# First batch in passes of 128, 128 and 320 rows, channel mix opened by two chunks of 128 rows: top-k attention with a channel mix on one Trainium2 core

## The chip, the cores and the metric

The kernel runs on one core of one Trainium2 chip. Five engines of the core matter here, each with its own queue of instructions: PE (TensorE: matrix products and transposes), ACT (ScalarE), DVE (VectorE), POOL (GpSimd), and SP (SyncE), which issues nearly all transfers. They meet only through semaphores. The metric is the device time of one execution in microseconds (us), lower being better. The profile is of one execution; its span runs from the first to the last instruction of the core.

## The reference, cut to what matters

```python
def _attn_ref(q, k, v):                     # each 8 batches x 8 heads x 576 rows x 64
    scores = (1 / np.sqrt(64)) * np.matmul(q, k.transpose(0, 1, 3, 2))
    kth = np.partition(scores, -32, axis=-1)[..., -32:-31]
    scores = np.where(scores >= kth, scores, -1000000000.0)
    attn = np.exp(scores - np.max(scores, axis=-1, keepdims=True))
    attn = attn / (np.sum(attn, axis=-1, keepdims=True) + 1e-09)
    return np.matmul(attn, v)

def _moe_ref(x, mu_k, mu_r, w_k, w_v, w_r):  # x: 8 x 576 x 512; w_k 512x1024, w_v 1024x512, w_r 512x512
    x_prev = ...                             # x moved down by one row, zeros in the first
    xk = mu_k * x + (1.0 - mu_k) * x_prev
    xr = mu_r * x + (1.0 - mu_r) * x_prev
    k = np.maximum(xk @ w_k, 0.0)
    v = k * k @ w_v
    r = 1.0 / (1.0 + np.exp(-(xr @ w_r)))
    return r * v
```

The output of the attention, its heads side by side, is the x of the channel mix. A row of x is complete only when all eight heads of its batch have given that row.

## The kernel before, in words

**Attention.** A batch has 576 query rows and eight heads in four head pairs. The unit of work is a tile: 128 query rows of one head against all 576 keys. Tiles 0 to 7 of a head pair are four blocks of 128 rows, each for the two heads in turn; tile 8 holds the last 64 rows of both heads. Eight batches, four head pairs and nine tiles make 288 tiles. `visits` (line 56) lists in what order they are taken: a batch is cut into passes (`HALVES`, line 52: tiles 0 to 3, then 4 to 8, so 256 and 320 rows; `EDGE`, line 53, can give other cuts for single batches and is empty), and a pass runs over the four head pairs. One head pair within one pass is a visit; there are 64.

A visit brings in on the SP queue the rows beyond 512 of the keys (`tl`), its query rows (`qn`) and the values (`v`, `vr`); the first visit of a head pair also loads and transposes the keys (`kn`, `K`), which are then held for its later pass. Transposes are done on PE (lines 934 and 948) and copied out by ACT (939 and 950). For a tile, PE makes scores (`score`, line 990, and `sliver`, 986), ACT copies them to `sc` (995), DVE looks for the 32 largest (`cand`, 1000 to 1005), ACT and POOL count (1020, 1022), DVE finds the eighth candidate and the threshold (1023, 1025), ACT exponentiates (1028), DVE masks and sums (`mask`, 1031). PE then transposes the masked scores (1036), ACT copies them (1038), and PE multiplies by the values (`weigh`, 1066 and 1067). For up to four tiles of a visit together, DVE inverts the sums (`inv`, 1077 and `inv2`, 1078), POOL spreads them (1084), PE and ACT turn them (1088, 1093), and DVE writes the rows of x (`place`, 1101 and 1103).

**Weights.** The three weight matrices come in 20 blocks of 128 x 512, all near the start: each is split into two parts of reduced precision by ACT, four DVE operations (`wclamp`, `wshift`, `wsign`, `wexp`, lines 1280 to 1284) and POOL; twelve also use PE (1293). The last ones, for w_v, end on POOL (1298).

**Channel mix.** The 4608 output rows are cut into chunks (`SIZES`, line 70: 18 chunks of 256). POOL and ACT mix a chunk with its shifted rows and split it (lines 1173 to 1187); PE then does `hidden` (8 pieces of 12 products, moving operand as wide as the chunk), `gate` (2 pieces of 6 products, 512 wide, for each 128 rows) and `value` (4 such pieces for each 128 rows). Line 703 to 705 are the three products of the helper `three` that all pieces use. ACT and POOL bring `hidden` out (1202 to 1207), ACT and POOL work on the gate (1220 to 1224), DVE joins gate and value (1238, 1239), and SP stores. The buffers `hh` and `hl` for the hidden layer exist once, so a chunk's values must be done before the next chunk's hidden layer is written. The pieces of all chunks are chained one behind the other on PE (`piece`).

**Order.** All operations are put down as a graph with costs, and a planner (`Plan.run`, line 242) writes out one order for each engine before the kernel is built. It takes the operation that can start first, and among those that can start nearly as soon the one with the lowest key. A key is the number of the tile to which the work belongs plus a constant for the kind of operation (`OFF`, with `HEAD` added below key 48 and `TAIL` above 252). The key of a chunk follows from the number of the tile that completes its rows:

```python
at, size = at + STEP * size / CH, n
r = max(ready[b, u] for b, s, m in pieces for u in units_of(b, s, m)) + min(LAG, LAG0 + c * LAG1)
at = max(at, r)
```

A piece is also held back (`pace`, with PACE = -2) until the scores of the tile two before its key have been put in order. Readiness is 15 for the first 256 rows of the first batch and 35 for its other rows; STEP is 15.812 and LAG 10.811. So the first chunk has the key 15 + 8.92 = 23.9, the second 35 + 10.811 = 45.8, the third 51 + 10.811 = 61.8.

Of the kernel before, what the change touches and what calls it, by code (L numbers as in the profile page):

```python
# [37 lines left out]
OFF = dict(kt=-21.382, kq=-14.248, rest=-18.039, v=-7.011, v8=8.546, tk=-6.103, ck=5.233, tq=-5.229, cq=-6.609, tr=-1.299, cr=-10.196, zero=24.959,  # L38
           score=-0.141, score8=-16.328, keep=-1.042, cand=4.797, best=-8.27, drop=-27.489, under=-2.864, nb=-4.48, count=2.291, below=0.265,
           eighth=6.343, nine=7.479, exps=3.115, mask=-0.613, turn=3.366, et=4.204, turnl=3.568, el=4.37, weigh=1.271, inv=3.182, inv2=-5.081,  # L40
           turni=-0.009, ri=0.848, place=-1.878, lowest=20.12, ranks=16.635, mu=-6.363, nmu=11.593, changek=8.781, sharek=-2.615, addk=-15.155,
           xhk=-0.563, xlk=-31.338, changer=-9.67, sharer=8.479, addr=2.956, xhr=5.904, xlr=-8.649, hidden=2.062, relu=-10.213, sq=4.638, r2=6.141,
           hl=-4.223, gate=1.884, gexp=5.081, ga=14.727, ln=-4.806, inv1=3.806, newton=-5.08, value=-0.042, scaled=-17.152, gated=-15.006,
           store=7.854, w=19.648, wabs=-0.882, wclamp=0.952, wshift=-8.969, wsign=-1.393, wexp=-0.548, wfine=1.179, whi=3.694, wmul=8.819,
           wsub=-8.872, wlo=4.08, spread=1.597, sliver=-4.179, low=2.901, lowt=-13.42, lowr=-9.695, lowc=-4.212, wcp=0.231)
CANDS, BESTS = 0.045, -0.62
LAG, STEP, WAT, WSTEP, GATE, VALUE, PACE = 10.811, 15.812, 0.678, 0.755, 7.749, 14.045, -2.0
# [36 lines left out]
HEAD = dict(sharek=3.354, ck=-3.568, zero=6.524, lowt=3.202, score8=0.214, ga=4.843, store=3.315, el=0.191, gate=0.108, wlo=0.364, tr=-0.131,  # L84
            turni=-1.056, sq=3.388, ln=-4.07, hl=-5.431, changer=2.017, relu=-14.934, wmul=-1.439, low=4.872, xhk=0.716, inv=2.094, v=4.81,
            gated=-1.266, xlk=12.101, turn=0.113, r2=0.637, xlr=-10.187, inv1=4.923, addr=1.519, ri=-4.935, below=-1.831, scaled=-5.097, best=-1.072,
            wabs=-0.847, lowr=-0.696, sliver=-1.103, tk=-0.128, nmu=-3.551, kq=3.958, changek=2.107, count=-0.05, hidden=-1.273, addk=-5.101,
            xhr=2.146, lowc=-0.428, cq=0.701, eighth=-1.645, w=1.074, nb=-2.325, kt=-7.062, wshift=-2.765, wexp=0.003, ranks=8.978, rest=-10,
            spread=5.051, mask=-0.34, whi=0.196, newton=-10.373, drop=-2.508, gexp=-0.274, keep=-0.268, tq=-0.017, inv2=3.214, mu=-5.036, weigh=0.017,
            cr=-1.986, turnl=0.004, score=-0.211, under=-2.424, v8=2.951, nine=0.151, place=1.785, sharer=3.985, et=0.015, wfine=-0.129, wsign=1.009,  # L90
            exps=-0.306, wsub=-1.021, lowest=-1.465, value=0.017, wcp=-0.278)
TAIL = dict(addr=0.853, cr=4.328, wshift=-2.172, wexp=-2.611, scaled=0.049, sq=2.406, lowt=1.029, sliver=-0.332, nb=2.118, whi=1.277, xlk=6.06,
            xhk=3.07, store=0.534, nine=0.364, best=-3.303, wclamp=-3.212, ck=-0.471, rest=7.98, lowr=3.739, ln=-0.612, hl=2.336, turni=-5.416,
            xhr=-5.491, relu=-1.983, kt=0.597, v8=1.982, drop=-9.156, gate=-0.048, score8=3.803, eighth=1.269, under=5.06, inv2=2.762, v=0.064,
            w=-0.347, wmul=-2.191, wfine=2.635, cq=-0.832, lowest=-2.842, gexp=0.175, score=0.034, sharek=-1.259, wabs=-0.36, exps=0.582, nmu=-3.842,
            below=0.883, changek=2.733, tr=2.248, lowc=-0.397, tq=-0.647, wsub=1.611, inv=-0.862, low=2.896, gated=1.923, turnl=-0.233, place=1.226,
            ri=-4.487, r2=5.335, weigh=1.024, spread=-7.381, kq=3.792, cand=0.342, value=0.124, hidden=-0.65, newton=5.24, changer=2.918, zero=1.577,
            ranks=-4.862, mu=2.617, count=2.536, mask=4.85, tk=1.419, wsign=0.085, xlr=3.997, wlo=-3.068, inv1=-0.011, keep=-0.009, addk=4.321,
            ga=1.91, el=0.034, sharer=-1.07, wcp=0.415, turn=-0.048)
# [1349 lines left out]
```

## Time and profile before

| | |
|---|---|
| median of 3 runs | 1239.97 us (1239.73 to 1240.59) |
| the profiled execution's own time | 1239.58 us |
| its span | 1238.0 us |
| mean granted clock of TensorE | 0.981 |
| busy shares of the span | PE 96%, DVE 91%, ACT 89%, POOL 79% |

The span is 1.58 us shorter than the execution's own time, which includes what lies before its first and after its last instruction. A row of the windows view gives, for each stretch of the span, the busy time of every engine with the number of its instructions, the granted clock of TensorE, the mean share of the 16 transfer engines in use and the rate. A row of the grouped lines gives source line, engine, operation, output and input, shape, count, busy time and mean duration, then the idle time just before them. A mask of line 1031 leaves two records for each tile, the operation and the read of its sum, so records there are halved to count tiles. The chain of waits follows the work that ended last back in time.

### The profile page before, as it was taken

The page shows a single profiled execution, that of the slowest core. Times are in us where ns is not written, and L with a number is a line of the kernel's source. Part 1 is how long each engine was busy: PE and PEld are TensorE (multiplying, and loading weights), DVE is VectorE, ACT ScalarE, POOL GpSimd, SP SyncE. Part 2 cuts the span into 40 slices and gives each one's busy share as a digit, 9 for nine tenths or more (in the row PEclk, how much of TensorE's full clock was granted, in tenths as well). Part 3 has the DMA queues.
Part 4 walks back from the last instruction along what each step waited for, and adds up shares of the span by engine and source line. Part 5 has one row for each costly group of instructions (what it writes and reads, how often), then busy time and mean ns, then how long its engine had stood idle before and what let it go on. Part 6 is the DMA issues. An engine that isn't in the chain of part 4 may idle for free.

```text
span 1238.0 us, 29646 instructions
## 1 busy us (share of the span) xinstructions
PE 1185.3 (96%) x9069; PEld 913.8 (74%) x9069; DVE 1132.4 (91%) x6217; ACT 1107.8 (89%) x2428; POOL 980.6 (79%) x872
## 2 busy tenths in 40 slices
PE   5876999999999999999999999999999999999997
PEld 3434777878777776778787877787878787878786
DVE  5999999999999999999999999999989998999711
ACT  6897899999999999999999999999999999999752
POOL 2568995887778877888789787979697969788895
PEclk8997799999999999999999999999999999999999
DMA  7233112111221122111121112111211121101000
GB/s 189 93 95 97 35 35 66 41 36 42 57 54 31 45 50 57 36 39 45 50 56 38 35 49 58 42 43 34 59 47 45 27 59 40 50 26 32 20 27 20
DMA packets 125512, 61.80 MB, mean 50 GB/s; under 512 B 101792, under 2 KB 118176, under 8 KB 125344
## 3 DMA queue, kind: packets, MB, share of 16 engines
q1 hardware_dynamic: 124656, 59.42, 17.8%
q8 instruction: 74, 1.21, 0.4%
q14 instruction: 94, 0.77, 0.2%
q10 hardware_dynamic: 688, 0.39, 0.1%
HBM read 50.34 MB, written 9.44 MB: 48 GB/s over the span
## 4 chain that ended last, share of the span: by engine, by line
PE 79%; DVE 9%; ACT 6%; issue 1%; POOL 0%; DMA 0%; SPq 0%; DVEq 0%; ACTq 0%
PE rot L703 13%; PE rot L705 12%; PE rot L704 12%; PE ps L1066 10%; PE rot L1036 9%; PE ps L990 9%; PE ps L986 2%; PE ps L1067 2%; PE ps L977 2%; PE rot L934 2%; DVE cand L1000 2%; DVE E L1031 2%; PE rot L1088 1%; ACT sc L995 1%; PE ps L1045 1%; ACT se L1028 1%
## 5 line engine op out<-in xcount | busy, mean ns | idle before, releaser
L1022 POOL TENSOR_TENSOR sg<-sc,sg 128x576 f32<-128x576 f32 x288 | 409.2, 1423 | 165.6 <-ACT sg L1020 161.9
L1000 DVE MAX8 cand<-sc 128x8 f32<-128x82 f32 (+1 forms) x2016 | 390.5, 231 | 10.6 <-ACT sc L995 9.9
L1020 ACT ACTIVATE sg<-sc,seen 128x576 f32<-128x576 f32 x288 | 225.9, 784 | 8.6 <-DVE seen L1012 7.2
L1031 DVE SCALAR_TENSOR_TENSOR E<-sc,seen,se 128x576 f32<-128x576 f32 x288 | 231.0, 802 | 0.5 <-DVE nine L1025 0.2
L1028 ACT ACTIVATE se<-sc,seen 128x576 f32<-128x576 f32 x288 | 217.6, 756 | 8.4 <-DVE E L1031 5.8
L1023 DVE MAX8 top<-sg 128x8 f32<-128x576 f32 x288 | 215.7, 749 | 9.7 <-POOL sg L1022 9.2
L995 ACT ACTIVATE sc<-ps 128x576 f32<-128x576 f32 x288 | 185.4, 653 | 27.8 <-DVE E L1031 11.4
L1036 PE MATMUL rot<-ident,E 128*128 128x128 f32 x1152 | 180.7, 280 | 12.7 <-DVE E L1031 5.1
L1038 ACT ACTIVATE et<-rot 128x512 f32<-128x512 f32 x288 | 173.9, 604 | 9.7 <-PE rot L1036 8.6
L1002 DVE MAX8 top<-cand 128x8 f32<-128x56 f32 x864 | 179.7, 208 | 2.1
L1036 PEld LDWEIGHTS rot<-ident,E 128*128 128x128 f32 x1152 | 133.4, 143 | 62.6 <-DVE E L1031 7.1
L703 PE MATMUL rot<-xh,wk 128*128 128x256 f32 x576 | 172.5, 299 | 0.4 <-ACT kd L950 0.4
L1066 PEld LDWEIGHTS ps<-et,v 128*64 128x64 f32 x2560 | 128.7, 138 | 54.5 <-ACT el L1047 17.9
L1066 PE MATMUL ps<-et,v 128*64 128x128 f32 (+1 forms) x2560 | 164.4, 271 | 3.0 <-ACT el L1047 2.7
L705 PE MATMUL rot<-xh,wk 128*128 128x256 f32 x576 | 162.4, 282 | 0.0
L704 PE MATMUL rot<-xl,wk 128*128 128x256 f32 x576 | 162.1, 281 | 0.0
L990 PE MATMUL ps<-K,qs 64*128 64x512 f32 x512 | 149.7, 662 | 0.7 <-ACT sc L995 0.6
L703 PE MATMUL rot<-wv,hh 128*128 128x512 f32 x288 | 123.3, 428 | 0.0
L1005 DVE MATCH_REPLACE8 cand<-top,cand 128x56 f32<-128x56 f32 x576 | 115.9, 201 | 0.0
L705 PE MATMUL rot<-wv,hl 128*128 128x512 f32 x288 | 113.7, 395 | 0.0
L704 PE MATMUL rot<-wv,hh 128*128 128x512 f32 x288 | 113.6, 394 | 0.0
L703 PEld LDWEIGHTS rot<-xh,wk 128*128 128x128 f32 x576 | 109.7, 190 | 5.0 <-issue 2.4
(115 smaller groups left out, 2723.0 us busy)
## 6 DMA issues: line engine op xcount, KB each, us to landing
v<-in_v SPq DMA_DIRECT2D x64, 256.0 KB, 2.8
out<-eb SPq DMA_DIRECT2D x35, 256.0 KB, 2.0
kn<-in_k SPq DMA_DIRECT2D x64, 128.0 KB, 2.8
qn<-in_q SPq DMA_DIRECT2D x126, 64.0 KB, 2.1
stage<-in_moe_w_k SPq DMA_DIRECT2D x8, 512.0 KB, 6.2
xT<-in_moe_w_v SPq DMA_DIRECT2D x8, 512.0 KB, 3.6
tl<-in_k SPq DMA_DIRECT2D x128, 16.0 KB, 2.0
vr_in<-in_v SPq DMA_DIRECT2D x128, 16.0 KB, 2.5
```

Source lines behind the costliest of these rows:

```text
L703: return [nc.tensor.matmul(ps, lhsT=sh, rhs=mh, start=first, stop=False), nc.tensor.matmul(ps, lhsT=sh, rhs=ml, start=False, stop=False), ...
L704: nc.tensor.matmul(ps, lhsT=sh, rhs=ml, start=False, stop=False),
L705: nc.tensor.matmul(ps, lhsT=sl, rhs=mh, start=False, stop=last)]
L990: return [nc.tensor.matmul(ps[h].t, lhsT=qs.t[w, c * 128:(c + 1) * 128], rhs=P.K.t[w], start=True, stop=True) for h, w in enumerate(ws)]
L1000: lambda T=T, c=c: nc.vector.max(T.cand.t[:, 8 * c:8 * c + 8], T.sc.t[:, CUTS[c]:CUTS[c + 1]]), reads=[T.sc], writes=[(T.cand, c)])
L1020: lambda T=T, sn=sn: nc.scalar.activation(T.side.t, T.sc.t, AF.Sign, bias=sn(T, 1), scale=-BELOW, accum_out=T.top.t[:, TOPK:TOPK + 1]),
L1022: plan.op(POOL, "below", n, 1375, 1430, lambda T=T: nc.gpsimd.tensor_mul(T.side.t, T.sc.t, T.side.t), reads=[T.sc], writes=[T.side])
L1023: plan.op(DVE, "eighth", n, 660, 754, lambda T=T: nc.vector.max(T.top.t[:, 24:32], T.side.t), reads=[T.side], writes=[(T.top, 3)])
L1028: plan.op(ACT, "exps", n, 667, 754, lambda T=T, pe=pe, sn=sn: nc.scalar.activation(pe.t, T.sc.t, AF.Exp, bias=sn(T, 0), scale=SCALE), read ...
L1031: lambda T=T, U=U, pe=pe, sn=sn: nc.vector.scalar_tensor_tensor(T.e(), T.sc.t, sn(T, 2), pe.t, op0=OP.is_ge, op1=OP.mult, accum_out=U.rs.t ...
L1036: return [nc.tensor.transpose(pt.t[:, c * 128:(c + 1) * 128], E.t[:, o + c * 128:o + (c + 1) * 128], ident) for c in range(NKC)]
L1066: return [*[nc.tensor.matmul(pa[hs[j]], lhsT=vs[j][:, c, :], rhs=ms[c][j], start=(c == 0), stop=False) for c in range(NKC) for j in range(2)],
```

## The change

The first batch is cut into three passes instead of two: tiles 0 and 1 (rows 0 to 127), tiles 2 and 3 (rows 128 to 255) and tiles 4 to 8 (rows 256 to 575), each over all four head pairs. That makes 68 visits in place of 64. The first 256-row chunk of the channel mix becomes two of 128 rows; the other 17 chunks keep their rows. All constants of the planner's keys are given anew for this, so the order on every engine is another one over the whole kernel. No operation gets another form beyond the sizes that follow from the cuts.

```diff
-OFF = dict(kt=-21.382, kq=-14.248, rest=-18.039, v=-7.011, v8=8.546, tk=-6.103, ck=5.233, tq=-5.229, cq=-6.609, tr=-1.299, cr=-10.196, zero=24.959,
...
+OFF = dict(kt=-22.637, kq=-11.82, rest=-20.526, v=-9.532, v8=9.111, tk=-5.962, ck=8.211, tq=-5.193, cq=-8.242, tr=-1.288, cr=-9.428, zero=26.367,
...
-CANDS, BESTS = 0.045, -0.62
-LAG, STEP, WAT, WSTEP, GATE, VALUE, PACE = 10.811, 15.812, 0.678, 0.755, 7.749, 14.045, -2.0
+CANDS, BESTS = 0.044, -0.596
+LAG, STEP, WAT, WSTEP, GATE, VALUE, PACE = 10.811, 15.812, 0.129, 0.92, 7.756, 14.051, -2.0
...
-EDGE = {}
+EDGE = {0: (range(0, 2), range(2, 4), range(4, 9))}
...
-SIZES = [256, 256, 256, 256, 256, 256, 256, 256, 256, 256, 256, 256, 256, 256, 256, 256, 256, 256]
+SIZES = [128, 128, 256, 256, 256, 256, 256, 256, 256, 256, 256, 256, 256, 256, 256, 256, 256, 256, 256]
...
-BONUS = {("S", "W"): -1.086, ("T", "W"): 3.287, ("R", "W"): 3.489, ("T", "S"): -0.028, ("R", "S"): -0.426, ("W", "S"): -1.169, ("S", "R"): 1.769, ("T", "R"): -0.968, ("W", "R"): 4.451, ("R", "R"): -0.294}
+BONUS = {("S", "W"): -1.286, ("T", "W"): 3.343, ("R", "W"): 3.487, ("T", "S"): 0.148, ("R", "S"): -0.304, ("W", "S"): -1.2, ("S", "R"): 1.763, ("T", "R"): -0.968, ("W", "R"): 3.166, ("R", "R"): -0.386}
...
-NEAR = dict(PE=182, ACT=165, DVE=28, POOL=271, SP=294)
+NEAR = dict(PE=182, ACT=165, DVE=28, POOL=267, SP=505)
...
-LWAT, LWSTEP = -2.585, 1.51
-LAG0, LAG1 = 8.92, 24.398
+LWAT, LWSTEP = -2.439, 1.485
+LAG0, LAG1 = 9.28, 19.088
...
-HEAD = dict(sharek=3.354, ck=-3.568, zero=6.524, lowt=3.202, score8=0.214, ga=4.843, store=3.315, el=0.191, gate=0.108, wlo=0.364, tr=-0.131,
...
+HEAD = dict(sharek=-2.489, ck=-6.619, zero=11.997, lowt=6.27, score8=1.224, ga=1.872, store=16.832, el=0.208, gate=-0.08, wlo=-0.016, tr=0.09,
...
-TAIL = dict(addr=0.853, cr=4.328, wshift=-2.172, wexp=-2.611, scaled=0.049, sq=2.406, lowt=1.029, sliver=-0.332, nb=2.118, whi=1.277, xlk=6.06,
...
+TAIL = dict(addr=-4.273, cr=4.021, wshift=-3.452, wexp=-4.841, scaled=4.193, sq=1.982, lowt=0.079, sliver=-8.219, nb=-5.556, whi=-0.937, xlk=8.216,
...
```

More of the change, by code (lines that the diff above doesn't have):

```diff
@@ L37 @@
 BIG = 3.0e38
-OFF = dict(kt=-21.382, kq=-14.248, rest=-18.039, v=-7.011, v8=8.546, tk=-6.103, ck=5.233, tq=-5.229, cq=-6.609, tr=-1.299, cr=-10.196, zero=24.959,
[L39 to L45, printed above, removed]
@@ L78 @@
 WINDOW, PHASE, WARM, COLD = 3413.0, 2079.0, 0.87, 0.58
-NEAR = dict(PE=182, ACT=165, DVE=28, POOL=271, SP=294)
+NEAR = dict(PE=182, ACT=165, DVE=28, POOL=267, SP=505)
 LAST, JOINT, PEAT = "last", True, 112
-LWAT, LWSTEP = -2.585, 1.51
-LAG0, LAG1 = 8.92, 24.398
+LWAT, LWSTEP = -2.439, 1.485
+LAG0, LAG1 = 9.28, 19.088
 WPE = 12
-HEAD = dict(sharek=3.354, ck=-3.568, zero=6.524, lowt=3.202, score8=0.214, ga=4.843, store=3.315, el=0.191, gate=0.108, wlo=0.364, tr=-0.131,
[L85 to L91, printed above, removed]
@@ L92 @@
-TAIL = dict(addr=0.853, cr=4.328, wshift=-2.172, wexp=-2.611, scaled=0.049, sq=2.406, lowt=1.029, sliver=-0.332, nb=2.118, whi=1.277, xlk=6.06,
[L93 to L99, printed above, removed]
+HEAD = dict(sharek=-2.489, ck=-6.619, zero=11.997, lowt=6.27, score8=1.224, ga=1.872, store=16.832, el=0.208, gate=-0.08, wlo=-0.016, tr=0.09,
+            turni=-1.957, sq=-2.744, ln=4.584, hl=-11.257, changer=3.109, relu=-14.215, wmul=1.015, low=13.241, xhk=4.504, inv=0.63, v=2.378,
+            gated=-6.033, xlk=19.736, turn=0.098, r2=7.625, xlr=6.041, inv1=5.892, addr=3.26, ri=-4.602, below=1.293, scaled=-2.104, best=2.34,
+            wabs=-2.653, lowr=-15.341, sliver=-1.315, tk=-1.739, nmu=1.364, kq=-2.115, changek=1.165, count=0.39, hidden=-0.946, addk=-16.072,
+            xhr=5.643, lowc=0.912, cq=1.236, eighth=-1.334, w=2.16, nb=-19.454, kt=-8.364, wshift=-7.503, wexp=-0.768, ranks=-0.573, rest=-8.761,
+            spread=3.633, mask=-3.1, whi=0.215, newton=-13.635, drop=6.545, gexp=0.8, keep=0.344, tq=0.603, inv2=-0.157, mu=-5.336, weigh=0.135,
+            cr=4.349, turnl=0.369, score=-0.122, under=1.423, v8=2.742, nine=0.052, place=3.564, sharer=2.346, et=0.018, wfine=0.496, wsign=1.149,
+            exps=-0.453, wsub=-2.521, lowest=-13.921, value=1.331, wcp=-11.617, cand=-0.022)
@@ new lines @@
+TAIL = dict(addr=-4.273, cr=4.021, wshift=-3.452, wexp=-4.841, scaled=4.193, sq=1.982, lowt=0.079, sliver=-8.219, nb=-5.556, whi=-0.937, xlk=8.216,
+            xhk=1.771, store=6.443, nine=-0.18, best=-1.616, wclamp=0.814, ck=-0.469, rest=7.277, lowr=2.974, ln=-7.81, hl=2.432, turni=-8.13,
+            xhr=-2.471, relu=0.278, kt=-4.493, v8=3.31, drop=-14.733, gate=0.303, score8=2.521, eighth=1.07, under=1.611, inv2=7.305, v=4.437,
+            w=1.208, wmul=-1.261, wfine=5.003, cq=-1.045, lowest=-1.352, gexp=-0.071, score=-0.026, sharek=-0.433, wabs=-4.683, exps=2.021,
+            nmu=-4.225, below=2.677, changek=0.13, tr=1.919, lowc=-2.236, tq=-0.583, wsub=-3.633, inv=-8.16, low=-0.806, gated=13.198, turnl=-0.195,
+            place=-1.505, ri=1.021, r2=2.891, weigh=1.447, spread=-10.049, kq=2.911, cand=-0.026, value=0.71, hidden=-0.005, newton=7.797,
+            changer=2.951, zero=4.963, ranks=-8.616, mu=-7.588, count=-0.664, mask=-2.56, tk=5.532, wsign=-0.027, xlr=4.181, wlo=-5.593, inv1=0.946,
+            keep=-1.135, addk=1.419, ga=-3.618, el=0.17, sharer=7.791, wcp=1.202, turn=-1.67, et=-2.455)
```

7 lines of the change are left out of this document (added).

## The prediction

> **What bounds the kernel now.** I read the page's slices first, then the busy times by stage, then how many tiles each stage finishes.
>
> ```profile
> PE   5876999999999999999999999999999999999997
> ...
> DVE  5999999999999999999999999999989998999711
> ...
> PEclk8997799999999999999999999999999999999999
> ```
>
> Each digit covers 31 us. DVE is full from the second slice on, PE only from the fifth. The last three slices belong to PE alone. So I cut the span at 30, 100, 137, 222 and 1166 us and asked the windows view (columns: stretch, its length, busy time with count of PE, PEld, DVE, ACT, POOL, then granted clock, transfer share, GB/s).
>
> ```profile
> 0.00:30.00 30.00, 16.53 (x58) 9.38 (x58) 17.43 (x88) 17.68 (x35) 6.70 (x17) 0.84 0.70 185
> 30.00:100.00 70.00, 54.63 (x278) 28.52 (x276) 69.41 (x290) 61.19 (x128) 43.05 (x36) 0.94 0.35 103
> 100.00:137.00 37.00, 26.30 (x151) 17.11 (x152) 36.05 (x169) 30.57 (x64) 31.75 (x28) 0.68 0.25 73
> 137.00:222.00 85.00, 83.11 (x672) 65.26 (x671) 83.79 (x478) 79.56 (x180) 69.72 (x62) 0.98 0.18 44
> 222.00:1166.00 944.00, 939.08 (x7507) 736.80 (x7507) 914.17 (x5173) 889.84 (x1971) 776.45 (x691) 1.00 0.16 43
> 1166.00:1232.00 66.00, 65.61 (x411) 56.78 (x409) 11.24 (x25) 28.93 (x55) 52.90 (x43) 1.00 0.06 21
> ```
>
> The same view for the masks alone (line 1031, DVE, two records a tile):
>
> ```profile
> 30.00:100.00 70.00, 9.12 (x23) 0.94 0.35 103
> 100.00:137.00 37.00, 5.42 (x14) 0.68 0.25 73
> 137.00:222.00 85.00, 18.66 (x46) 0.98 0.18 44
> 222.00:1166.00 944.00, 197.69 (x488) 1.00 0.16 43
> ```
>
> Three regimes follow. From 30 to 222 us DVE bounds: it idles 0.59, 0.95 and 1.21 us in the three stretches, 2.75 us together. PE idles 37 - 26.30 = 10.7 us from 100 to 137, at a clock of 0.68. From 137 to 222, 23 tiles take 85 us, 3.70 us each. From 222 to 1166, 244 tiles take 944 us, 3.87 each, with PE idle for only 4.9 us and DVE for 29.8: there PE bounds. After 1166 the rest of the mix runs on a full PE.
>
> The mix begins here (source view: count, min/median/max duration, first and last start; then the first product of the second chunk in the timeline):
>
> ```profile
> L703 PE MATMUL rot<-xh,wk x576: 277/281/562, 136.7 to 1214.3; 128*128 128x256 f32 x192
> ```
>
> ```profile
> 209.92 0.38 PE L703 MATMUL rot<-xh,wk 128*128 128x256 f32 x1 [0.37 <-ACT kd L950]
> ```
>
> Chunk 0 thus fills PE from 137 us on, and chunk 1 starts at 210 us, about where its key 45.8 less the pace of 2 puts it.
>
> **The change part by part.** *Keys.* By the rule quoted above the prediction, the two small chunks get the keys 7 + 9.28 = 16.3 and 15 + 10.811 = 25.8 where the one had 23.9. The chunk with rows 256 to 511 keeps 45.8 (readiness 35), and so does every later one. So nothing of the mix after about 210 us moves against the tiles. The gain from starting early, if there is one, must come before that point, where DVE bounds.
>
> *PE.* I need the price of a product with 128 moving columns. The first two rows are neighbours of a hidden piece at full clock, the next two of a value piece (timeline, starts first), the last two the chain's time for four transposes and for one float32 product with 128 columns (both halves of it).
>
> ```profile
> 139.91 0.28 PE L703 MATMUL rot<-xh,wk 128*128 128x256 f32 x1
> 140.03 0.28 PE L704 MATMUL rot<-xl,wk 128*128 128x256 f32 x1
> ```
>
> ```profile
> 200.56 0.40 PE L703 MATMUL rot<-wv,hh 128*128 128x512 f32 x1
> 200.79 0.39 PE L704 MATMUL rot<-wv,hh 128*128 128x512 f32 x1
> ```
>
> ```profile
> 142.51 0.44 PE rot L1036 x4
> 144.92 0.22 PE ps L986 x2
> ```
>
> Start to start: 0.12 us for 256 columns, 0.23 for 512. For 128 columns the ends are half of the first, 0.06, and 0.22, the float32 product. I take 0.11, a transpose's 0.44 / 4, because it too loads 128 x 128 new weights for 128 columns. A 256-row chunk costs 96 x 0.12 + 24 x 0.23 + 48 x 0.23 = 28.1 us. A 128-row one costs 96 x 0.11 + 12 x 0.23 + 24 x 0.23 = 18.8 us. Two make 37.7, so PE gets 9.6 us more to do, and four more transposes of key rows, 0.44 us. Of chunk 0, hidden and gate (10.6 + 2.8 = 13.3 us) can run before 137 us; I leave its values after it, since they need w_v. Free there is 10.7 us at the clock of 0.68, so at least 7.3 us of full-speed work. At full clock today's 26.3 us would shrink to about 17.9 and leave 19.1. I take 13.3 as moved. What is left for 137 to 222 is 24.4 us against 28.1 now: PE is relieved there by 3.7 us, while DVE sets the pace.
>
> For the spacing of matrix products there is a page of the Trainium skill, "TensorE: Matmul & The Clock Gate", section "Back-to-back issue gap": a stream of weight loads with 128-column products is given about 81 ns a product. By it the two half chunks would cost 5.6 us less on PE; since DVE bounds that stage, the sum would stay as it is. No run here has shown such a product yet.
>
> *DVE.* Four more visits close four more groups.
>
> ```profile
> L1101 DVE TENSOR_TENSOR xT<-ps,ri 128x256 f32<-128x256 f32 x64 | 26.6, 416 | 3.2 <-PE ps L1067 0.9 <-POOL xm L1183 0.8 <-PE ps L1045 0.6
> L1078 DVE RECIPROCAL rs<-rot 128x4 f32<-128x4 f32 x64 | 10.6, 166 | 0.0
> L1077 DVE TENSOR_SCALAR rot<-rs 128x4 f32<-128x4 f32 x64 | 10.1, 158 | 0.6 <-ACT qs L939 0.4
> L1103 DVE TENSOR_TENSOR xT<-ps,ri 128x64 f32<-128x64 f32 x32 | 7.0, 218 | 2.2 <-ACT ri L1094 1.0 <-PE ps L1067 0.4 <-ACT sc L995 0.4
> ```
>
> Four times 0.158 + 0.166 is 1.3 us. A placement of 128 columns is, between 218 ns for 64 and 416 for 256, about 284 (an estimate); eight of them in place of four of 416 add 0.6. Together 1.9 us, all before 137 us, on the engine that bounds. Gate and value work on DVE stays at one pair for each 128 rows.
>
> In return PE is lighter from 137 on and earlier warm, so part of DVE's 2.75 us of waiting can go: at least nothing, at most all. I take two thirds, 1.8 us, because most of it lies after 100 us, where PE changes.
>
> *ACT, POOL, SP.* For each new visit ACT gets a copy of key rows at 0.279 us, and its copy of 256 query columns at 0.388 becomes two of 128, near 0.279 each.
>
> ```profile
> L939 ACT ACTIVATE qs<-rot 128x256 f32<-128x256 f32 x63 | 24.4, 388 | 2.0 <-PE rot L934 1.5
> L950 ACT ACTIVATE kd<-rot 128x128 f32<-128x128 f32 x32 | 8.9, 279 | 2.1 <-PE rot L948 1.9
> ```
>
> That is 4 x 0.45 = 1.8 us, and about as much again for the split mix, against 8.8 + 6.4 us of idle ACT from 30 to 137. Cost: nothing; without that cover, up to 4 us. SP issues four more sets of transfers:
>
> ```profile
> 9.54 0.47 SPq L920 DMA_DIRECT2D v<-in_v  x1
> 10.05 1.12 SPq L923 DMA_DIRECT2D vr_in<-in_v  x2
> 12.61 1.21 SPq L915 DMA_DIRECT2D tl<-in_k  x2
> ```
>
> At 2.8 us a visit this is 11 us of issue within the first 100, beside the weights' 20 blocks, which queue on SP too. Key loads of the four head pairs are wanted after two tiles each instead of four. I take nothing. The ends are -1 us (the first query load is half as large) and +3 us (a weight block or a key tile late while transfers are at 0.70 in the first 30 us). POOL is a rival below.
>
> *Sum.* Against the execution's own time: 1239.58 + 1.9 - 1.8 = 1239.7, and 0 for the stretches from 222 us on, whose keys and PE work are unchanged. The median lies 0.4 above that execution: **1240.0 us**, no change. For the new constants I take nothing either: no row prices another order. Their ends are bounded in the first rival.
>
> **The rivals.** *The new order carries the PE-bound stretch better (faster).* If its 244 tiles went at the 3.70 us of the stretch before, they would take 903 us, 41 less. So there is much to win from a better interleaving, and every constant differs. Against it: no cut touches that stretch, and a new order can lose as well. A tenth of the 41 gives 1236. Chance 0.31.
>
> *The clock (faster).* This row follows a gap of PE in the slow stretch (start, duration, what; idle before it):
>
> ```profile
> 111.63 2.07 PE L977 MATMUL ps<-K,kd 128*128 128x512 f32 x2 [4.60 <-ACT sc L995]
> ```
>
> If filling such gaps brings the clock from 0.68 to 1, the 26.3 us of PE from 100 to 137 shrink by 8.4; if all of it came through, 1240.0 - 8.4 = 1231.6. Against it, DVE idles only 0.95 us there. Chance 0.03. The Trainium skill, "TensorE: Matmul & The Clock Gate", section "What's actually happening", says that the clock halves after an idle window of some 3.4 us and recovers after a busy one; the trace's 0.68 beside that gap agrees.
>
> *POOL runs over (slower).* Chunk 0's POOL work now comes while POOL still finishes w_v.
>
> ```profile
> L1207 POOL TENSOR_TENSOR hl<-r,hh 128x512 fp32r<-128x512 f32 x72 | 92.6, 1286 | 5.2
> L1187 POOL TENSOR_TENSOR xl<-xm,xh 128x512 fp32r<-128x512 f32 x72 | 92.4, 1288 | 9.2 <-ACT xh L1185 8.7
> L1206 POOL TENSOR_TENSOR r<-r 128x512 f32<-128x512 f32 x72 | 74.9, 1040 | 14.9 <-ACT hh L1204 14.7
> ...
> L1183 POOL TENSOR_TENSOR xm<-xm,xT 128x512 f32<-128x512 f32 x48 | 57.0, 1189 | 6.6 <-ACT xm L1178 6.5
> ...
> L1173 POOL TENSOR_TENSOR xd<-xT 128x512 f32<-128x512 f32 x24 | 25.0, 1044 | 2.0 <-DVE rot L1077 1.1 <-DVE xT L1101 0.9
> ...
> L1183 POOL TENSOR_TENSOR xm<-xm,xT 128x256 f32<-128x256 f32 x16 | 10.7, 693 | 0.0
> ```
>
> Preparation and hidden layer of 256 rows cost 2 x 1.044 + 4 x 1.189 + 4 x 1.288 + 4 x (1.040 + 1.286) = 21.3 us. At half size an operation costs 693 / 1189 = 0.58 of that: 12.4 us. POOL idles 5.25 us from 100 to 137, so up to 7.1 spill onto the product of line 1022, which every tile waits for ahead of line 1023, and onto w_v. The queue behind them holds chunk 1, since PE's pieces are chained. It decides from the point where chunk 0's work adds more than 5.25 us there; as part of that preparation stands there already, I take half the overflow, 3.5 us: 1243.5. Chance 0.14.
>
> *Short products at the float32 rate (slower).* At 0.22 us a half chunk costs 10.6 more. Chunk 0 has room for most of it; chunk 1 would take the 3.7 us of relief and 1.9 of idle PE, and 5 us would be left: 1245. It decides above 0.11 + 5.6 / 96 = 0.17 us. Chance 0.07.
>
> *The mix doesn't start earlier.* If the small chunk waits until 137 anyway, the 9.6 us fall on the PE of 137 to 222, less its 1.9 idle: about 1247.7. Chance 0.05.
>
> **How the numbers follow.** No change has 0.40, with a range of its own from 1237.5 to 1242.5: 0.2%, or 2.5 us, is about what a measurement of this kernel can tell from none. Faster has 0.31 + 0.03 = 0.34, slower 0.14 + 0.07 + 0.05 = 0.26. The range of 1233.5 to 1246.5 leaves out the clock case, the late mix, and the outer parts of the first and third rivals, some 0.18.
>
> **What would show it.** Right: the first hidden product between 85 and 110 us with 0.11 between starts; DVE at 98% from 30 to 222; the first product of the chunk from row 256 at 210 within 3 us; the distance from there to the end unchanged. The order rival would show a shorter distance there. The clock rival shows that product 6 us or more early, POOL's and the short products' a late one, with DVE waiting at line 1023 in the one and starts 0.2 us apart in the other. I would be wrong above all if the stretch from 222 us on changes by itself.

## The result and the profile after

| | before | changed |
|---|---|---|
| median of 4 runs | 1239.85 us (1239.25 to 1240.59) | 1250.5 us (1247.48 to 1252.51) |
| ratio, 95% interval | | 1.0081 (1.0067 to 1.0096) |
| the profiled execution's own time | 1239.58 us | 1247.48 us, the lowest of its four |
| its span | 1238.0 us | 1245.7 us |

The changed kernel is slower by 10.7 us, 0.8%, and its runs lie 5 us apart where those of before lie 1.3 apart. The forecast was no change. The profile shows the best of the four executions, so it holds 7.7 of the 10.7 us.

The page of the changed kernel, the slices of 31 us each:

```profile
PE   5877998999999999999999999999999999999998
...
DVE  6999999999999999999999999999989998999611
...
PEclk7998899999999999999999999999999999999999
```

At this grain hardly anything has moved; the loss is too small for it. The windows view of the changed kernel, with the columns of the prediction:

```profile
0.00:30.00 30.00, 16.63 (x57) 9.80 (x59) 17.62 (x100) 17.37 (x37) 7.43 (x18) 0.81 0.59 146
30.00:100.00 70.00, 57.32 (x282) 30.29 (x281) 67.84 (x276) 64.61 (x141) 44.35 (x43) 0.91 0.40 123
100.00:137.00 37.00, 30.12 (x199) 24.09 (x199) 34.99 (x164) 29.50 (x65) 34.12 (x34) 0.86 0.30 85
137.00:222.00 85.00, 78.84 (x659) 59.23 (x657) 81.60 (x462) 76.97 (x182) 66.19 (x66) 0.98 0.19 47
222.00:1166.00 944.00, 939.22 (x7515) 737.65 (x7514) 918.54 (x5192) 889.28 (x1973) 771.22 (x688) 1.00 0.16 43
```

The same view for the masks alone:

```profile
30.00:100.00 70.00, 8.91 (x22) 0.91 0.40 123
100.00:137.00 37.00, 5.63 (x14) 0.86 0.30 85
137.00:222.00 85.00, 16.31 (x41) 0.98 0.19 47
222.00:1166.00 944.00, 199.13 (x491) 1.00 0.16 43
```

From 30 to 222 us DVE now idles 2.16, 2.01 and 3.40 us: 7.57 together, where it was 2.75. From 137 to 222, 41 mask records stand where 46 stood. PE has more to do from 100 to 137 (30.12 for 26.30, at a better clock) and then idles 6.16 us from 137 to 222, where it idled 1.89. From 222 to 1166 the stretch takes in three records more than before.

The 48th mask, found by counting the masks in the timeline, stands behind both small chunks' hidden layers. In before, then in the changed kernel (start, duration, what):

```profile
239.04 0.80 DVE L1031 SCALAR_TENSOR_TENSOR E<-sc,seen,se 128x576 f32<-128x576 f32 x1
```

```profile
245.57 0.80 DVE L1031 SCALAR_TENSOR_TENSOR E<-sc,seen,se 128x576 f32<-128x576 f32 x1
```

It is 6.5 us late. The source view (first and last start) gives the last mask, again before and then after:

```profile
L1031 DVE SCALAR_TENSOR_TENSOR E<-sc,seen,se x288: 791/802/816, 18.8 to 1166.9; 128x576 f32<-128x576 f32 x144
```

```profile
L1031 DVE SCALAR_TENSOR_TENSOR E<-sc,seen,se x288: 787/802/817, 18.4 to 1171.8; 128x576 f32<-128x576 f32 x144
```

So the tiles lose 6.5 us up to the 48th, win 1.7 back from there to the 288th (which is 4.8 late), and the work behind the last mask takes 73.9 us for 71.1. That is 6.5 - 1.7 + 2.8 = 7.6, but for rounding the 7.7 between the spans. Behind the last mask PE is busy 68.58 us where it was 64.67, so more of its work is left for the end. Up to the 48th mask DVE waits 4.4 us more than in before and works 2.1 us more; that is the 6.5. The point matters, for the distance moves: counted in the same way, the 16th mask is 2.3 late, the 24th 2.3, the 36th 9.0, the 73rd 9.8, the 250th 8.7. So the loss arises in the head, and from the 73rd to the 250th tile the two kernels go at much the same pace.

The largest step is from the 24th to the 36th mask. The windows view of DVE alone from the one to the other, before and then after:

```profile
149.77:193.52 43.75, 43.02 (x244) 1.00 0.14 36
```

```profile
152.06:202.56 50.50, 47.68 (x266) 1.00 0.23 59
```

Of the 6.8 us DVE waits for 2.1 (2.82 idle for 0.73). The other 4.7 it works on 22 more instructions, which in before stand at other places of its list: candidates of other tiles and a gate and value pair. The twelve tiles behind win 2.5 of this back.

What DVE waits for in the changed kernel, 137 to 222 us (waits view: us, times, longest), and the longest of these waits in the timeline:

```profile
DVE cand L1000 <- ACT sc L995: 1.8, 2, 1.5
DVE xT L1103 <- ACT el L1047: 0.4, 1, 0.4
```

```profile
177.80 0.83 DVE L1000 MAX8 cand<-sc 128x8 f32<-128x82 f32 x5 [1.48 <-ACT sc L995]
```

That copy stands behind other work on ACT. In the timeline of the changed kernel:

```profile
174.63 0.90 ACT L1178 ACTIVATE xm<-xd,mu 128x256 f32<-128x256 f32 x2
175.43 0.37 ACT L950 ACTIVATE kd<-rot 128x256 f32<-128x256 f32 x1
175.70 0.77 ACT L1020 ACTIVATE sg<-sc,seen 128x576 f32<-128x576 f32 x1
...
176.46 0.74 ACT L1028 ACTIVATE se<-sc,seen 128x576 f32<-128x576 f32 x1
177.12 1.18 ACT L995 ACTIVATE sc<-ps 128x576 f32<-128x576 f32 x2
```

The copy also needs the scores of the last keys (`sliver`, line 986), and these need the key rows of line 950. PE makes them last:

```profile
176.23 0.38 PE L986 MATMUL ps<-kd,qs 128*128 128x128 f32 x2
```

So of what stands ahead on ACT, the mixing (1178, by its 256 columns that of the chunk from row 256, not of a half chunk) can hold up line 950, and the exponentiation (1028) the copy itself. DVE stood for 1.48 us. The engines' lists don't meet at that point. The waiting in this stage is of this form; how much of the 1.48 us each of the two made wasn't tried.

### The profile page after: what moved, and what is told of

Read it like the earlier page. It is cut to its first block, busy times and chain, and to the rows that moved or that the text cites. A ratio compares the mean times of both kernels' runs of the same rounds, so it can differ in the third digit from the quotient of the medians.

```text
span 1245.7 us, 29947 instructions
## 1 busy us (share of the span) xinstructions
PE 1196.5 (96%) x9169; PEld 924.9 (74%) x9169; DVE 1136.6 (91%) x6229; ACT 1113.6 (89%) x2460; POOL 984.0 (79%) x894
## 4 chain that ended last, share of the span: by engine, by line
PE 78%; ACT 11%; DVE 7%; POOL 1%; issue 1%; DMA 1%; SPq 0%; DVEq 0%; ACTq 0%; POOLq 0%
PE rot L703 12%; PE rot L705 12%; PE rot L704 12%; PE ps L1066 10%; PE rot L1036 9%; PE ps L990 9%; PE rot L934 2%; PE ps L986 2%; PE ps L1067 2%; PE ps L977 2%; ACT sg L1020 2%; ACT sc L995 2%; ACT se L1028 2%; PE rot L1088 1%; DVE cand L1000 1%; ACT et L1038 1%
## 5 line engine op out<-in xcount | busy, mean ns | idle before, releaser
L1020 ACT ACTIVATE sg<-sc,seen 128x576 f32<-128x576 f32 x288 | 226.4, 786 | 10.5 <-DVE seen L1012 9.1
L1036 PE MATMUL rot<-ident,E 128*128 128x128 f32 x1152 | 179.4, 279 | 11.3 <-DVE E L1031 5.4
L703 PE MATMUL rot<-xh,wk 128*128 128x256 f32 (+1 forms) x608 | 180.9, 298 | 2.1 <-ACT kd L950 1.4
L705 PE MATMUL rot<-xh,wk 128*128 128x256 f32 (+1 forms) x608 | 171.0, 281 | 0.0
L1066 PEld LDWEIGHTS ps<-et,v 128*64 128x64 f32 x2560 | 129.4, 138 | 55.7 <-ACT el L1047 19.9
L704 PE MATMUL rot<-xl,wk 128*128 128x256 f32 (+1 forms) x608 | 170.7, 281 | 0.0
L703 PE MATMUL rot<-wv,hh 128*128 128x512 f32 x288 | 123.8, 430 | 0.4 <-ACT kd L950 0.4
L703 PEld LDWEIGHTS rot<-xh,wk 128*128 128x128 f32 x608 | 115.8, 190 | 4.5 <-ACT kd L950 1.9
L704 PEld LDWEIGHTS rot<-xl,wk 128*128 128x128 f32 x608 | 115.8, 190 | 0.1
L705 PEld LDWEIGHTS rot<-xh,wk 128*128 128x128 f32 x608 | 115.3, 190 | 0.0
```

The lines of the kernel that those rows point to most:

```text
L703: return [nc.tensor.matmul(ps, lhsT=sh, rhs=mh, start=first, stop=False), nc.tensor.matmul(ps, lhsT=sh, rhs=ml, start=False, stop=False), ...
L704: nc.tensor.matmul(ps, lhsT=sh, rhs=ml, start=False, stop=False),
L705: nc.tensor.matmul(ps, lhsT=sl, rhs=mh, start=False, stop=last)]
L1020: lambda T=T, sn=sn: nc.scalar.activation(T.side.t, T.sc.t, AF.Sign, bias=sn(T, 1), scale=-BELOW, accum_out=T.top.t[:, TOPK:TOPK + 1]),
L1036: return [nc.tensor.transpose(pt.t[:, c * 128:(c + 1) * 128], E.t[:, o + c * 128:o + (c + 1) * 128], ident) for c in range(NKC)]
L1066: return [*[nc.tensor.matmul(pa[hs[j]], lhsT=vs[j][:, c, :], rhs=ms[c][j], start=(c == 0), stop=False) for c in range(NKC) for j in range(2)],
```

## The experiments

Each edit below is against the kernel before or the changed one, as named. "Behind" is the start of a mask against the same mask in the profile of before. The medians of before beside these runs were 1239.4 to 1239.7 us. Profiles show one execution of each, and among the profiles in the changed kernel's order (further down) the 48th mask lies from 6.1 to 10.8 us behind, so small differences in these columns say little.

| | median us | ratio, interval | 48th mask behind | 288th |
|---|---|---|---|---|
| passes alone, constants of before | 1240.05 | 0.9993 to 1.0012 | +2.5 | +1.7 |
| half chunks alone, constants of before | 1258.28 | 1.0142 to 1.0176 | +8.1 | +16.9 |
| both, constants of before | 1259.63 | 1.0148 to 1.0182 | +12.0 | +19.4 |
| neither, new constants | 1252.5 | 1.0091 to 1.0124 | +3.1 | +9.3 |
| passes alone, new constants | 1254.99 | 1.0106 to 1.014 | +4.1 | +13.4 |
| half chunks alone, new constants | 1257.93 | 1.013 to 1.0163 | +12.0 | +15.6 |
| before, `cand` moved by 0.03 | 1249.08 | 1.0057 to 1.0091 | +5.2 | +10.8 |
| before, `score` moved by 0.029 | 1251.25 | 1.0077 to 1.011 | 0.0 | +11.3 |
| changed, `cand` moved by 0.03 | 1261.39 | 1.0156 to 1.019 | +12.4 | +24.0 |
| changed, `weigh` moved by 0.04 | 1262.04 | 1.0165 to 1.0199 | +10.7 | +19.9 |

**The parts apart.** First the two cuts with the constants of before, and the new constants without the cuts or without the half chunks.

```diff
-EDGE = {}
+EDGE = {0: (range(0, 2), range(2, 4), range(4, 9))}
...
-SIZES = [256, 256, 256, 256, 256, 256, 256, 256, 256, 256, 256, 256, 256, 256, 256, 256, 256, 256]
+SIZES = [128, 128, 256, 256, 256, 256, 256, 256, 256, 256, 256, 256, 256, 256, 256, 256, 256, 256, 256]
```

Both edits, on before:

> The three passes and the two half chunks, planned with the constants of before. Theory A (the cuts cost: dearer half chunks packed into half the tiles, and more small DVE work in the first 100 us): slower than before by 6 to 12 us, and the 36th mask some 8 us or more later than before's 193.5 us. Theory B (the new constants cost, the cuts are harmless): within 2.5 us of before.

Both undone, on the changed kernel:

> The cuts of before (two passes, 18 chunks of 256), planned with the new constants. Theory A: within 3 us of before. Theory B: slower than before by 7 to 11 us.

Only the second undone, on the changed kernel:

> The new constants and the three passes, but 18 chunks of 256 rows. Theory A: only the small DVE work of the four added visits is left, so 2 to 3 us over before (1242 to 1243), and the 36th mask within 4 us of before. Theory B: as slow as the changed kernel, 1248 to 1251. A third theory, that POOL's load from chunk 0 at 100 to 150 us costs: as theory A, since chunk 0 then waits for row 255.

They gave 1259.63, 1252.5 and 1254.99. Cuts and constants don't add up: the cuts under the old constants cost 20.2 us, the constants without the cuts 13.1, and both together 10.7. All three lose more than any of their theories forecast. Each half of the change is bad without the other, and "what do the cuts cost" has no answer until the price of an order is known.

**The price of another order.** A kernel with the same instructions in another order shows it, so one constant was moved by a trifle.

```diff
-           score=-0.141, score8=-16.328, keep=-1.042, cand=4.797, best=-8.27, drop=-27.489, under=-2.864, nb=-4.48, count=2.291, below=0.265,
+           score=-0.141, score8=-16.328, keep=-1.042, cand=4.767, best=-8.27, drop=-27.489, under=-2.864, nb=-4.48, count=2.291, below=0.265,
```

> The kernel before with one constant of the keys moved by 0.03 (cand 4.797 to 4.767, the new constants' value) and nothing else: the same cuts and work, another order over the whole kernel. Theory R: 5 us or more slower than before, most of it lost little by little after 222 us. Theories A and P say that orders of the same work are alike: within 2.5 us of before.

The second moves `score` from -0.141 to -0.17 in before:

> A second new order of the work of before: score moved from -0.141 to -0.17, nothing else. Theory R (a new order of the same work costs, the order of before fits better than its neighbours): 1246 to 1253. If the first such kernel was a bad draw: under 1243.

The same two kinds of step away from the changed kernel, `cand` from 4.767 to 4.797, and `weigh` from 1.231 to 1.271:

> A new order of the changed kernel's work: cand moved from 4.767 back to 4.797, nothing else. Theory R1 (the cuts cost nothing, the changed kernel is one more ordinary order): 1247 to 1254, as the new orders of the work of before. Theory R2 (the cuts cost some 8 us, and the constants planned for them hide most of that): 1255 to 1262, and at the 48th mask 8 us or more behind before.

> A second new order of the changed kernel's work: weigh moved from 1.231 to 1.271 (the old value), nothing else. As for the first: R1 1247 to 1254, R2 1255 to 1262.

All four lost 10 to 12 us against the kernel that they were moved from: 9.6 and 11.9 from before, 10.9 and 11.5 from the changed kernel. The second is the clearest: its first 48 tiles run as in before, and then it loses 11.3 us. Its windows:

```profile
137.00:222.00 85.00, 80.67 (x660) 62.23 (x661) 83.72 (x476) 79.25 (x179) 69.59 (x62) 1.00 0.17 44
222.00:1166.00 944.00, 935.09 (x7447) 730.52 (x7445) 911.16 (x5138) 881.32 (x1953) 768.43 (x685) 1.00 0.16 43
```

PE gets through 7447 instructions from 222 to 1166 us where before had 7507, and idles 8.9 us where before idled 4.9. No single wait stands out; it falls behind in several steps (4.5 us at the 100th mask, 6.2 at the 200th, 10.3 at the 250th). So in the stretch that the forecast put down as unchanged, a shifted order costs 5.6 to 11.6 us. The kernel before and the changed one both have an order that avoids this loss: from the 48th mask to the 288th before takes 927.9 us and the changed kernel 926.2; the four shifted ones take 5.6 to 11.6 more than before.

With the price known, like can be compared with like. The three orders with both cuts under other constants than the change gives them (1259.63, 1261.39, 1262.04) have a mean of 1261.0; the three without cuts under other constants than those of before (1249.08, 1251.25, 1252.5) have 1250.9. The cuts cost 10 us there, as they do between the two kernels themselves (9 with the spread keys further down, 1258.13, as a fourth).

**Which of the two cuts.** Each alone, with the constants of before, and the half chunks alone with the new ones:

> The three passes alone, with the constants of before: a second order for the passes' price. New orders of the work of before took 1249.1, 1251.3 and 1252.5. If the passes cost 2 to 4 us: 1252 to 1256. If nothing: 1248 to 1252.

> The two half chunks alone, with the constants of before: a second order for their price without the third pass. If they cost 5 us or more: 1255 to 1260. If nothing: 1248 to 1252.

> The changed kernel with two passes in the first batch instead of three, the two half chunks kept: both wait for row 255. The new constants with the old cuts gave 1252.5, with three passes alone 1255.0. If the half chunks by themselves cost (R2): 4 us or more over 1252.5, so 1256 to 1260. If they cost nothing (R1): 1250 to 1255.

The passes alone cost nothing (10 runs, 1240.05), less than either case of their expectation. Masks are 2.5 us late at the 48th tile, where DVE is 2.2 us busier, and 1.7 at the 288th. From about the 70th tile on, DVE's instructions stand again in the order of before, so here the planner fell back into the old order, and with it kept the fit: not every new plan costs. The half chunks alone end 18 to 19 us above before under either set of constants. If 10 to 12 of these are the lost order, as in the four runs above, 7 to 9 are their own price, and their masks show it early: the 48th is 8 and 12 us late. The windows of the half chunks with the new constants:

```profile
137.00:222.00 85.00, 83.88 (x680) 67.76 (x680) 75.05 (x422) 73.45 (x173) 64.90 (x69) 0.95 0.12 32
```

Here PE is full (1.1 us idle) and DVE idles 9.95 us: without the earlier pass the small chunk's first product comes at 132.6 us, and both half chunks fall into this stage.

**The work in a fixed order.** In the next runs every instruction keeps its place in the lists and only its size is cut, so the order is exactly that of the kernel named. First two of three products of the hidden layer are left out for chunk 0 of before, to see whether PE bounded before there; they are missing from that part of the channel mix.

```diff
-    return [x for h in range(HP) for x in three(ph.t[:, e * CH:e * CH + n], wk[0][:, h, w], wk[1][:, h, w], xh.t[:, h, :n], xl.t[:, h, :n], h == 0, h == HP - 1)]
+    return [nc.tensor.matmul(ph.t[:, e * CH:e * CH + n], lhsT=wk[0][:, h, w], rhs=xh.t[:, h, :n], start=h == 0, stop=h == HP - 1) for h in range(HP)] if c < 1 else [
...
```

> The kernel before with its order untouched; the hidden layer of its first chunk keeps one product of three, so 7.7 us of PE work leave 137 to 160 us. If PE does not bound there, as the prediction has it, the time stays within 2 us and the 36th mask within 1.5 us of 193.5; if PE bounds, both come 4 to 8 us earlier.

It gave 1240.35 (0.9995 to 1.0014), and the 36th mask came 1.3 us earlier: PE's time there didn't set the kernel's time. The same edit for both half chunks (`c < 2`) of the changed kernel, and of the half chunks alone with the new constants:

> The changed kernel with its order untouched; the hidden layer of the two half chunks keeps one product of three, so 7 us of PE work leave each of them. Theory A (from 140 to 190 us the dear half chunks crowd attention out of PE): the masks 24 to 36 come back to 45 to 46 us for the twelve (50.5 in the changed kernel, 43.8 before), and the time falls by 4 to 7 us, to about 1245. Theory P (POOL is what holds 100 to 160 us): no change at the 36th mask within 1.5 us. Theory R (what costs is that any new order fits the chip less well than the old one): no more than 2 us gained.

> The kernel with two passes and two half chunks, its order untouched; the hidden layer of the half chunks keeps one product of three, so 7 us leave each on PE. If the half chunks' price without the third pass is PE time (there PE idles 1.1 us and DVE 10 us from 137 to 222): the 48th mask comes 5 to 8 us earlier and the time falls from 1257.9 to about 1251. If it is the doubled small work on ACT and POOL or the order: within 2 us of 1257.9.

In the changed kernel 8.5 us less of PE gave 1248.96, 1.5 us less, within its scatter, and the masks of the profile stayed where they were (48th +6.6, 288th +4.9). Its window shows the freed time turned into idle PE, 11.7 us of it:

```profile
137.00:222.00 85.00, 73.34 (x579) 51.81 (x573) 80.70 (x460) 77.11 (x181) 65.13 (x64) 0.96 0.19 47
```

With the half chunks alone, where PE was full, it gave 1254.94 for 1257.93, and the 48th mask came 4.2 us earlier (+7.8 for +12.0). That is between the two cases of the expectation. The whole gain lies ahead of the 24th mask (+0.4 for +5.5). There PE's time was a part of the price.

GpSimd's turn in the changed kernel: sum (1183), square (1206) and gate (1221, 1224) of both half chunks on one column, the rest of these columns left as it stands. Then ScalarE's: the gate chain of both and mixing, splitting, relu and square of the second (1178, 1185, 1202, 1204). Last all three engines together, with both subtractions of the second (1187, 1207). A part of one line of each kind:

```diff
-lambda rr=rr, n=n: nc.gpsimd.tensor_mul(rr.t[:, :, :n], rr.t[:, :, :n], rr.t[:, :, :n])
+lambda rr=rr, n=1 if c < 2 else n: nc.gpsimd.tensor_mul(rr.t[:, :, :n], rr.t[:, :, :n], rr.t[:, :, :n])
...
-def relu(ph=ph, rr=rr, n=n):
+def relu(ph=ph, rr=rr, n=1 if c == 1 else n):
```

> The changed kernel with its order untouched; for the two half chunks POOL's additions, squares and gate operations work on one column, so some 14 us leave POOL between 95 and 190 us. Theory P: the 24th to 36th masks come 4 us or more earlier and the time falls by 4 us or more. Theory A: less than 2 us at the 36th mask and in the time. Theory R: less than 2 us.

> The changed kernel in its own order, every instruction and wait in its place, with ScalarE's work for the two half chunks cut to one column (gate chain of both; mixing, splitting, relu and square of the second), so about 11 us of ScalarE time less between 100 and 222 us; that part of the channel mix is left out of the result. In the changed kernel the masks fall behind those of before by 6.8 us between the 24th and the 36th tile, and VectorE waits there for score copies that stand behind this work on ScalarE. If ScalarE's time is what costs: the 36th mask moves from 9.0 us behind to at most 4, the 48th from 6.5 to at most 3, and the time from 1250.5 to about 1246. If the order itself costs, whatever the work in it: 48th mask still 5 to 8 us behind, time 1248 to 1251.

> The same, and the half chunks' TensorE time (first product of three in the hidden layer) and GpSimd time (sum, square, gate, Newton step of both; both subtractions of the second) cut as well, in the same order; this work is left out of the result. The half chunks then cost little more than their places in the order. If their work on the three engines together is what holds the tiles back, though none alone does: 48th mask at most 3 us behind before, time 1244 to 1247. If the order costs whatever the work in it: 48th mask still 5 to 8 us behind, time 1247 to 1250.

GpSimd's gave 1250.07 and ScalarE's 1250.14 (1248.52 to 1250.99): nothing. ScalarE's cut was smaller than its expectation said, 4.5 us of busy time and not 11, so it excludes only that much. It also leaves the mixing ahead of DVE's longest wait from 137 to 222 us, which is the 256-row chunk's; that wait is 1.2 us there. All together gave **1246.36** (1245.67 to 1247.19; ratio 1.0036 to 1.0069). Its windows:

```profile
100.00:137.00 37.00, 27.68 (x147) 20.05 (x149) 35.02 (x167) 30.01 (x67) 31.58 (x34) 0.71 0.30 87
137.00:222.00 85.00, 75.39 (x595) 54.32 (x591) 81.48 (x460) 72.89 (x183) 54.18 (x66) 0.94 0.19 47
```

POOL has 12 us less to do from 137 to 222, PE 3.5 and ACT 4.1, and DVE idles 3.52 us there as in the changed kernel (3.40). Its 48th mask:

```profile
245.17 0.80 DVE L1031 SCALAR_TENSOR_TENSOR E<-sc,seen,se 128x576 f32<-128x576 f32 x1
```

Still 6.1 us behind, as the case of the order had it; the time falls as the other case had it. So that delay isn't paid for the work that was cut. It goes with the order and with what was left in place: the fixed cost of the small instructions, gate and value products, and the added visits' work on DVE, which with the passes alone made 2.5 us at the 48th mask and nothing of the time. Together this is 1246.36 - 1239.66 = 6.7 us of the time; that most of it is the order is concluded from what the cuts left, not shown by a run of its own. What the cut work is worth, 1250.5 - 1246.36 = 4.1 us, can't be seen by the two profiles, since that of the changed kernel is its lowest execution (1247.48) and this one the highest of its four (1247.19).

**Where the scatter comes from.** The profile of the run with ScalarE's cut is one of the later executions: its 48th mask is 8.8 us behind. In both, PE has gaps of 1.2 to 1.3, 1.5 and 1.0 to 1.3 us from 110 us on, and takes up the half chunk's products again at 118.8 and at 118.6 us. From there on PE's windows differ (stretch, length, busy, clock, transfers); first the changed kernel, then ScalarE's cut:

```profile
118.00:124.00 6.00, 4.74 (x39) 1.00 0.15 31
124.00:131.00 7.00, 5.79 (x36) 0.51 0.12 50
```

```profile
118.00:124.00 6.00, 5.51 (x27) 0.50 0.20 51
124.00:131.00 7.00, 7.00 (x38) 0.50 0.08 33
```

Much the same gaps ahead, another clock. In the second the products of the half chunk go at half speed (PE timeline, 0.21 us apart where the changed kernel has 0.11):

```profile
122.29 0.42 PE L703 MATMUL rot<-xh,wk 128*128 128x128 f32 x1
122.50 0.41 PE L704 MATMUL rot<-xl,wk 128*128 128x128 f32 x1
122.72 0.41 PE L705 MATMUL rot<-xh,wk 128*128 128x128 f32 x1
```

Tiles wait behind them. DVE's placement of a finished group stands for 2.01 us in the changed kernel, and here for 3.72:

```profile
132.71 0.29 DVE L1103 TENSOR_TENSOR xT<-ps,ri 128x128 f32<-128x128 f32 x1 [3.72 <-PE ps L1067]
```

Where two thirds of the products are left out (PE's cut alone, and all three) the same placement waits 0.3 us although the clock is 0.50 from 118 to 124 in both; where GpSimd's cut leaves them in, it waits 4.1 us and the 48th mask is 10.8 behind. So in these profiles, one execution each, half-chunk products at half clock push the tiles. All of it happens early: at the 24th mask the five profiles in this order are 1.3 to 6.5 us behind, the two without the products least (1.3 and 1.6). From there to the 36th each loses 6.5 to 7.7 us, whatever was cut; that step belongs to the order. That the half clock is the whole of the changed kernel's scatter isn't shown: PE's cut alone still had runs from 1247.26 to 1250.66.

The Trainium skill, "TensorE: Matmul & The Clock Gate", section "What's actually happening", says that the clock is set by activity in a window of some 3.4 us that runs free, so that one kernel can meet it in different phases. The two clocks after so similar gaps agree with it, though these are two kernels, equal in order and not in ACT's work.

**The plan and the keys.** Two tries to get the head's loss back. The first leaves the products out as above and tells the planner so (a part of the line); the order is planned anew.

```diff
-piece("hidden", key(f + e), 12 * max(111.7, 10.7 + n * 0.418), hid,
+piece("hidden", key(f + e), (4 if c < 2 else 12) * max(111.7, 10.7 + n * 0.418), hid,
```

> The changed kernel's cuts and constants with one product of three in the half chunks' hidden layers, and the planner told of it, so it is a new order; to be held against the two new orders of the changed kernel's work, 1261.4 and 1262.0, and against the three passes without half chunks, 1255.0. If the planner passes the half chunks' PE time on to the attention: 1253 to 1257. If the price is in the other engines' doubled work: 1259 to 1263.

The second spreads the second half chunk's pieces over as many tiles as a whole chunk's:

```diff
-key = lambda x, at=at, n=n: at + x * STEP * n / CH / 20
+key = lambda x, at=at, n=CH if c == 1 else n: at + x * STEP * n / CH / 20
```

> The changed kernel with one edit: the second half chunk's keys are spread over 15.8 tiles instead of 7.9. Theory A: the 24th to the 36th mask lose no more than 2 us against before (they lose 6.7 now), and the time falls by 3 to 5 us, to about 1246. Theory B and the POOL theory: no change against the changed kernel, within 2 us of 1250.

The first gave 1255.06 (1.0097 to 1.0131), 6 to 7 us below the shifted neighbours of the changed kernel and at the level of the passes alone under the new constants, 1254.99. Its 48th mask is 13.9 behind all the same, so it won behind the head, by a way that this run doesn't show. The second gave 1258.13 (1.0125 to 1.0159), 10.8 behind at the 48th mask. It is one more order, and its price fits those above; what the spreading itself is worth can't be told from it. No run here beat the kernel before.

## Why the prediction was wrong

**"DVE's waiting", -1.8 us, is the step that failed**, in sign. DVE idles 4.8 us more from 30 to 222, not 1.8 less; up to the 48th mask it is 4.4 of the 6.5 us, and the rest is more busy time. The reason given, a lighter PE from 137 on, doesn't hold. Before didn't wait for PE there (1240.35 with PE relieved), and in the changed order relieving PE left the 36th and 48th masks where they were (9.0 and 6.6 behind). DVE's waiting came from what the in-order lists have ahead of a needed operation: up to 131 us the half chunk's products on PE (2.01 us), up to 178 us other work on ACT (1.48 us).

**"For the new constants I take nothing" and "0 for the stretches from 222 us on"** came out nearly right in size, but the first had no measurement behind it. From the 48th mask to the end the kernel loses 1.1 us (-1.7 and +2.8). That is luck as far as the prediction goes: four orders from nearly the same constants lose 5.6 to 11.6 us from the 48th mask to the 288th, and the same cuts under the constants of before cost 20.2 us in all instead of 10.7. The prediction saw that constants matter, as a rival that was priced only as a gain (1236, chance 0.31). What had to be asked was whether the new order reaches the fit of the old one. It does from the 73rd tile on, and not in the head.

**The median's distance from the profiled execution, +0.4 us,** was taken over from before. In the changed kernel it is 1250.5 - 1247.48 = 3.0, a part of the miss that no stretch of its profile shows. Of the 10.5 us between forecast and result, 6.2 are thus DVE's waiting (4.4 for -1.8), 2.6 this distance and 1.1 the work behind the 48th mask; the rest is small.

**PE's 9.6 us.** Size and price were about right: PE is busy 11.2 us longer, as the pages of before and after have it,

```profile
PE 1185.3 (96%) x9069; PEld 913.8 (74%) x9069; DVE 1132.4 (91%) x6217; ACT 1107.8 (89%) x2428; POOL 980.6 (79%) x872
```

```profile
PE 1196.5 (96%) x9169; PEld 924.9 (74%) x9169; DVE 1136.6 (91%) x6229; ACT 1113.6 (89%) x2460; POOL 984.0 (79%) x894
```

and the products stand 0.11 us apart at full clock (PE timeline of the changed kernel):

```profile
153.62 0.27 PE L705 MATMUL rot<-xh,wk 128*128 128x128 f32 x1
153.73 0.28 PE L703 MATMUL rot<-xh,wk 128*128 128x128 f32 x1
153.84 0.27 PE L704 MATMUL rot<-xl,wk 128*128 128x128 f32 x1
```

From 137 to 222 us PE is busy 4.3 us less, where 3.7 was forecast, though fewer tiles are in it. What the sum left out is what the moved products do to the tiles behind them: they go into a stretch whose clock was 0.68, and at half clock they take 0.21 us each. With other work taken out beside it, this part is worth up to the 4.1 us between 1250.5 and 1246.36.

**DVE's 1.9 us for four more groups** was about right: with the passes alone DVE is busy 1.4 us longer (1132.4 to 1133.8), and the last mask comes 1.7 later. The time didn't follow (+0.5, within measurement). That fits the last slices of the page, which belong to PE; it wasn't tried apart.

**The signs.** Right: the mix starts early, its first hidden product at 99.8 us.

```profile
L703 PE MATMUL rot<-xh,wk x608: 272/281/456, 99.8 to 1223.0; 128*128 128x256 f32 x136, 128*128 128x128 f32 x16
```

Wrong: DVE is at 96% from 30 to 222, not 98%, and the chunk from row 256 starts 12 us late, at 222.15 where 210 within 3 was forecast (PE timeline). Its key is unchanged, but by the pace rule it waits for tiles, which are late, and it follows the second half chunk in PE's chain. From there to the end it is 1023.6 us, where before had 1028.1 and no change was forecast. By the prediction's signs a shorter distance speaks for the order rival, but here it comes from a chunk that is 12 us late among tiles that are 6.5 late, and the time rose.

```profile
222.15 0.36 PE L703 MATMUL rot<-xh,wk 128*128 128x256 f32 x1
```

**The rivals.** The late product was named as POOL's sign, and the slower case had its chance there. Its size (1243.5) falls short and its mechanism doesn't hold: with that work on POOL cut the time stays at 1250.07, and no wait of DVE at line 1023 stands among those that the waits view lists from 100 to 222 us. The short products run at 0.11 at full clock, so not at the float32 rate. The mix did start early. The clock rival is refuted as a gain: the clock from 100 to 137 rose from 0.68 to 0.86 and the 24th mask came no earlier, but 2.3 us late. The clock did matter, in the other direction: where it was low it cost.

**What stays open.** Why the changed order holds the masks back from the 24th to the 36th tile: it isn't the half chunks' time on PE, on POOL or on ACT that was cut, though a part of that work stayed. What is left above all is where the lists put the pieces: DVE has other work ahead of the masks (4.7 us) and waits 2.1 us more. Single waits such as the 1.48 us show how, but no run rearranged that stretch alone. The five other orders with both cuts all lost more than the changed kernel; whether one that is chosen better would lose less wasn't tried.

## What to carry to other kernels

Before a change that needs a new plan is credited or charged with anything, plan the old work anew from slightly shifted constants and time that: here this alone costs 10 to 12 us, as much as the whole change. (Look whether the order really is another one: with the passes alone it fell back into the old one, and nothing was lost.) Then compare chosen orders with chosen ones and arbitrary ones with arbitrary ones. Work that is moved into an engine's idle time is priced at the clock of that place, and in fixed in-order lists it delays whatever stands behind it even if the engine as a whole has room.

## What the runs showed of the hardware that was not expected

- The granted clock can differ after much the same gaps of PE: 1.00 in one profile and 0.50 in the other from 118 to 124 us, which makes 0.11 or 0.21 us of each product with 128 columns.
- Halving the moving columns saved next to nothing: 0.11 us start to start for 128, 0.12 for 256. Cutting a 256-row chunk in two nearly doubles its hidden layer on PE.
- DVE's busy time depends on the order: the same 6217 instructions are busy 1132.4 us in before and 1137.0 in the kernel with `score` moved. What makes them longer wasn't looked into.
